# Gated mix of a recurrent memory attention and a 32-head attention: turns by transposing DMAs, zero products, paced weights, transfers issued by GpSimd

## The chip, the cores and the metric

One core of a Trainium2 chip. Its engines run their own instruction streams, in order, and meet at semaphores: TensorE (PE, with its weight loads PEld), VectorE (DVE), ScalarE (ACT), GpSimd (POOL) and SyncE (SP); transfers issued by SP, ACT or POOL run on the core's 16 DMA engines. The metric is the device time of one execution in microseconds, lower is better, as a median over runs.

## The reference

All inputs and the output are bfloat16.

```python
x = A_x                                            # [1, 2048, 576]
g = sigmoid((x * gate_w).sum(-1, keepdims=True))
return g * A(x) + (1 - g) * B(x)

def A(x):            # 64 segments of 32 rows, 32 heads of 128, memory of 8 rows
    mem = mem0
    for s in range(64):
        h = concat([mem, x[32*s : 32*s+32]])       # 40 rows x 576
        q, k, v = h @ Wq, h @ Wk, h @ Wv           # each 40 x (32 heads x 128)
        p = softmax(mask(q k^T / sqrt(128)))       # 40 x 40 for each head; memory rows see all
        o = (p v) @ Wo                             # 40 x 576
        mem = o[:8]                                # the next segment needs it
        out[s] = o[8:]

def B(x):            # 2048 rows, 32 heads of 18, no mask
    q, k, v = split(x @ wqkv)
    return softmax(q k^T / sqrt(18)) v @ wo
```

Both attentions work on `A_x`; `B_x` is not used. A is a recurrence: segment s+1 starts from eight rows that segment s ends with. B has no recurrence.

## The kernel before, in words

**Three stages.** (1) *Head*: x is loaded and turned, B's Q, K and V are projected (`project_qk` L528 on, `project_v`), evicted from PSUM and stored to DRAM in the layouts in which they are read back (`qtd`, `ktd`, `vgd`, `L561`, `L597`), while GpSimd loads A's weights wv, wq, wk (L478 and L481) in twelve chunks of 1 MB, each behind the one before the last. Then come the first 24 "last units" (`last_unit`, L803 and L807): the projections of the last 8 rows of 16 segments at once, which do not depend on the recurrence; their results are stored to `vld` and `qkd` (L841, L844). (2) *Segments*: the 64 steps of the recurrence, between whose instructions PE and ACT also do B's attention. (3) *Tail*: the last output products and stores.

**A segment.** The 8 memory rows and 24 of the x rows, 32 columns in all (`ht`), are multiplied with Wq, Wk, Wv in six units of 20 products (L1028; two halves of the heads for each), evicted to `tm` (L363). Q and K have to be turned, so that the head dimension lies on partitions: 16 PE transposes into a PSUM bank (L1087) and a DVE copy into `qk` (L1095). V goes to `v_sb` by eight small DMAs (L1067). GpSimd puts the 8 rows of the last units into `qk` (L997) and the next x rows into `ht` (L983 to L985). Then for each half: scores `psh` (L1108), exponent on ACT (L1118), mask, row sums `pss` (L1134), reciprocal, its broadcast `prb` (L1151), normalisation, `pso` (L1172), copies to `ot`, and 64 products with Wo into `acc` (L946). The memory rows of `acc` are cast (L1203, L1206), turned by three products `pw` (L1219 to L1221) and copied into the next `ht` (L1227).

**A visit** is one step of B's attention, 512 in all: scores `sb` of 128 keys and 512 queries of four heads (L708), their exponent `etb` on ACT (L717), and the product with V into `ob` (L726). Every 16 visits `ob` is normalised and stored. K, Q and V chunks are reloaded from DRAM through rings (`kch`, `qch`, `vch`, helper `by_head` L649).

**The order of the work** is set by a planner (`Plan`): every operation has an engine or two, a duration, dependences, a priority from the table `RANK`, and tokens for buffers; `run` simulates the engines and `choose` picks for each engine the ready operation of the best priority. The program is then written out in that order, so each engine's stream is fixed when it is built. `seg_gate` ties the visits to the segments: the first `RANK["ahead"]` visits may run before segment 0.

Of the kernel before, what the change touches and what calls it, by code (L numbers as in the profile page):

```python
# [17 lines left out]
    "switch": 0.289, "near": 0.006, "early": 0.149, "wait": 0.21, "Q0": 1.449, "K0": 1.44, "Q1": 1.668,  # L18
# [4 lines left out]
    "behind": 2, "tail": 0.042,  # L23
# [21 lines left out]
class Plan:  # L45
# [5 lines left out]
    SWITCH = 0.1  # L51

    def __init__(self):
        self.ops = []
        self.tokens = {}
        self.now = None
        self.lanes = [0.0] * self.LANES
        self.moved = 0.0

    def transfer(self, op):  # L60

        step = (op.end - op.start) / op.dmas
        for j in range(op.dmas):
            issued = op.start + (j + 1) * step
            self.moved = max(self.moved, issued + 0.9) + op.kb / op.dmas / 300.0
            self.lanes.append(max(self.moved + 1.0, self.lanes[-1]))
# [31 lines left out]
    def run(self):  # L98
# [12 lines left out]
        n = len(self.ops)  # L111
        best = {}
        dirty = set(free)
        while len(order) < n:
# [10 lines left out]
            est, op = best[pick]  # L125
            waiting_engs = op.engs
# [6 lines left out]
            if pick == "PE":  # L133
                if op.mode != mode:
                    dur += self.SWITCH
                mode = op.mode
            op.end = est + dur
            free[pick] = op.end
            if op.dmas:
# [20 lines left out]
    def choose(self, e, ops, now, mode):  # L160
        found = []
        for op in ops:
# [5 lines left out]
            if op.dmas:  # L168
# [47 lines left out]
def kernel(  # L216
# [37 lines left out]
    HD = H * Dh  # L254
    CT = 32
# [16 lines left out]

    const = ctx.enter_context(tc.tile_pool(name="const", bufs=1))
# [11 lines left out]
    nc.vector.memset(cap[:], 3.0e38)  # L285
    nc.vector.memset(bsel[:], 0.0)
# [24 lines left out]
    vgd = dpool.tile([GB, P, NKB * P], BF16, name="vgd")  # L311
    otd = dpool.tile([Dm, S], BF16, name="otd")
    vld = dpool.tile([n_seg * LO, HD], BF16, name="vld")
    qkd = dpool.tile([n_seg // SG, P, SG, 2, H * LO], BF16, name="qkd")
# [3 lines left out]
    def weights(name):  # L318
        return (
            aw1.tile([P, NF, HD], BF16, name=name + "_m"),  # L320
# [5 lines left out]
    def w_slice(w, c, f0, n):  # L326
        if c < NF:
            return w[0][:, c, f0:f0 + n], c
# [8 lines left out]
    wo7 = bint.tile([P, Dm], BF16, name="wo7")  # L337
# [50 lines left out]
    z_w7 = zero("zw7", wo7[:], 0.6, 4.0)  # L388
# [83 lines left out]
    weight_loads = {}  # L472
    chain = [wbl[-1], wbl[-1]]
    for w, src, name in ((wv, A_Wv, "wv"), (wq, A_Wq, "wq"), (wk, A_Wk, "wk")):
        w2 = src.rearrange("d h e -> d (h e)")
        for c in range(NF):
            def load_w(e, w=w, w2=w2, c=c):
                nc.gpsimd.dma_start(out=w[0][:, c, :], in_=rows(w2, c))  # L478
                for two in range(2):
                    o = TL * two + TR * c  # L480
                    nc.gpsimd.dma_start(  # L481
                        out=w[1][o:o + TR, :],
                        in_=w2[RW * c + P:RW * c + RW, two * (HD // 2):(two + 1) * (HD // 2)],
                    )

            chain.append(add(f"{name}{c}", "POOL", 2.1, load_w, [chain[-2]], prio=0.15, tail=8.5))
        weight_loads[name] = chain[-4:]
# [8 lines left out]
    gwl = add("gw", "POOL", 5.0, load_gw, [chain[5]], prio=0.9, tail=3.0)  # L496
# [35 lines left out]
    def project_qk(which, m, t, prio):  # L532
# [20 lines left out]

        def st(e):
# [15 lines left out]
    def project_v(hf, kb, prio):  # L570
# [24 lines left out]

        def st(e):
            dma(  # L597
                out=vgd[:, :, :].rearrange("g p (k f) -> k p g f", f=P)[kb][:, hf * GB // 2:(hf + 1) * GB // 2, :],
                in_=vt[:, :, :].rearrange("p (g j) e -> p g (j e)", j=4),
# [839 lines left out]
```

## Time and profile before

| | |
|---|---|
| time, median of 3 runs | 1567.85 us (1562.02 to 1577.5) |
| the profiled execution's own time | 1573.35 us |
| its span, first to last instruction | 1571.6 us |
| PE / ACT / DVE / POOL busy | 1425.7 / 1066.2 / 764.9 / 194.4 us |
| mean granted TensorE clock | 0.961 |
| first and last `pw` product (one for each of 63 segment ends) | 190.1 and 1514.0 us |

How to read it: a row of the page's part 5, or of the groups by line, is `line engine operation out<-in shapes xcount | busy, mean ns of one | idle time before, and what ended it`. A window row has for each engine its busy us and, in brackets, its instruction count, then the granted clock (1.00 is full speed), the DMA engines' busy share and GB/s. A timeline row is `start us, duration us, engine, line, operation, out<-in, forms, xcount, [idle before <-what ended it]`. "SPq" is SyncE's queue: it issues DMAs and is never counted as busy. Matmuls overlap their neighbours, so what one costs PE is best read from start to start.

### The profile page before, as it was taken

To read this page: it belongs to the slowest core of one execution; us is meant where nothing else is said; L and a number is where in the kernel's file an instruction comes from. 1 tells how busy PE (TensorE), PEld (TensorE's weight loads), DVE (VectorE), ACT (ScalarE), POOL (GpSimd) and SP (SyncE) were. 2 spreads that over 40 slices of the span, in tenths; PEclk is the share of its full clock that TensorE was granted. 3 is DMA by queue.
4 is the path that set the end of the run, shared out by engine and by line. 5 is a ranking of instruction groups with operands and counts; after the bars stand their busy time and mean duration, and the time that the engine had idled before them with its cause. 6 is when DMAs were issued, how large, how long until landed. Compare 5 with 4: busy or idle time off the path is not lost.

```text
span 1571.6 us, 68445 instructions
## 1 busy us (share of the span) xinstructions
PE 1425.7 (91%) x30582; PEld 813.4 (52%) x30582; DVE 764.9 (49%) x1604; ACT 1066.2 (68%) x809; POOL 194.4 (12%) x523
## 2 busy tenths in 40 slices
PE   5398999999999999999999999999999898988996
PEld 3154545555554545555555555555555454555555
DVE  5154555544545454545554544555444545443454
ACT  2121788877777777777777777777776767766771
POOL 7301000000000000010000000000110100000025
PEclk9599999999999999999999999999999999998998
DMA  9957411212222111222221112212131111111033
GB/s 319 287 152 206 68 44 51 56 33 45 42 49 49 32 44 53 56 43 46 39 50 44 42 43 52 57 39 41 38 76 37 34 34 40 33 32 31 26 106 97
DMA packets 246877, 104.83 MB, mean 67 GB/s; under 512 B 186487, under 2 KB 242039, under 8 KB 245047
## 3 DMA queue, kind: packets, MB, share of 16 engines
q1 hardware_dynamic: 241591, 80.40, 21.2%
q0 software_dynamic: 3840, 18.88, 3.5%
q8 instruction: 239, 3.92, 1.0%
q10 hardware_dynamic: 1152, 1.18, 0.3%
q14 instruction: 55, 0.45, 0.1%
HBM read 52.74 MB, written 30.86 MB: 53 GB/s over the span
## 4 chain that ended last, share of the span: by engine, by line
PE 72%; ACT 10%; DMA 7%; issue 4%; SPq 3%; DVE 3%; POOL 1%; ACTq 0%; DVEq 0%; POOLq 0%
PE pvv L1028 24%; PE acc L946 11%; PE sb L708 10%; ACT etb L717 9%; PE ob L726 8%; PE pt L1087 4%; PE pv L807 4%; DMA v_sb<-tm 3%; SPq L1067 2%; PE pq L539 2%; PE pso L1172 2%; PE pv L803 2%; PE psh L1108 1%; POOL wv_m L1349 1%; PE prb L1151 1%
## 5 line engine op out<-in xcount | busy, mean ns | idle before, releaser
L717 ACT ACTIVATE etb<-sb 128x2048 bf16<-128x2048 f32 x512 | 961.3, 1878 | 386.3 <-PE sb L708 328.2
L363 DVE CAST tm<-pvv 128x512 bf16<-128x512 f32 x352 | 242.6, 690 | 285.2 <-PE pvv L1028 270.9
L1028 PEld LDWEIGHTS <-ht 128*32 128x32 bf16 x7680 | 199.5, 96 | 186.9 <-DVE ht L1227 23.8
L708 PE MATMUL sb<-qch,kch 32*128 32x512 bf16 x2048 | 208.6, 391 | 28.9 <-ACT etb L717 18.0
L726 PE MATMUL ob<-etb,vch 128*32 128x512 bf16 x2048 | 207.4, 396 | 0.8 <-ACT etb L717 0.7
L946 PE MATMUL acc<-wo,ot 128*32 128x144 bf16 x8192 | 167.7, 245 | 10.9 <-issue 10.7
L946 PEld LDWEIGHTS <-ot 128*32 128x32 bf16 x8192 | 157.1, 107 | 22.2 <-issue 17.2
L1028 PE MATMUL pvv<-wk_m,ht 128*32 128x512 bf16 x2048 | 140.8, 380 | 18.3 <-DVE ht L1227 18.2
L1028 PE MATMUL pvv<-wq_m,ht 128*32 128x512 bf16 x2048 | 144.4, 380 | 0.0
L708 PEld LDWEIGHTS <-kch 32*128 32x128 bf16 x2048 | 65.1, 91 | 139.9 <-issue 109.3
L1028 PE MATMUL pvv<-wv_m,ht 128*32 128x512 bf16 x2048 | 133.9, 379 | 0.0
L983 POOL COPY ht<-xg 128x96 bf16<-128x96 bf16 x64 | 17.1, 267 | 859.7 <-PE pvv L1028 843.2
L363 DVE CAST ot<-pso 128x320 bf16<-128x320 f32 x197 | 90.0, 485 | 65.1 <-PE pso L1172 64.8
L1095 DVE COPY qk<-pt 128x1024 bf16<-128x1024 bf16 x128 | 87.8, 686 | 53.8 <-PE pt L1087 53.5
L726 PEld LDWEIGHTS <-vch 128*32 128x32 bf16 x2048 | 54.3, 93 | 112.6 <-issue 105.0
L1203 DVE CAST obf<-acc 128x144 bf16<-128x144 f32 x64 | 19.7, 307 | 169.4 <-PE acc L946 169.2
L1087 PEld LDWEIGHTS <-tm 128*128 128x128 bf16 x1024 | 57.5, 98 | 45.5 <-issue 27.1
L1087 PE MATMUL pt<-ident,tm 128*128 128x128 bf16 x1024 | 79.4, 220 | 0.0
L1172 PE MATMUL pso<-et,v_sb 64*128 64x40 bf16 x2048 | 54.7, 179 | 26.0 <-DVE ot L363 16.8
L1161 DVE TENSOR_TENSOR et<-et,prb 128x320 bf16<-128x320 bf16 x128 | 57.2, 483 | 23.8 <-PE prb L1151 22.1
L1172 PEld LDWEIGHTS <-v_sb 64*128 64x128 bf16 x2048 | 38.8, 94 | 56.3 <-DMA v_sb<-tm 29.0
L1247 POOL COPY otl<-ot 128x256 bf16<-128x256 bf16 x64 | 26.2, 409 | 328.2 <-DVE ot L363 187.8
(128 smaller groups left out, 1523.1 us busy)
## 6 DMA issues: line engine op xcount, KB each, us to landing
v_sb<-tm SPq DMA_DIRECT2D x512, 32.0 KB
qkd<-vl SPq DMA_DIRECT2D x64, 128.0 KB
xl<-qkd SPq DMA_DIRECT2D x64, 128.0 KB
wo<-in_A_Wo_dram POOLq DMA_DIRECT2D x4, 1152.0 KB, 11.3
wv_m<-in_A_Wv_dram POOLq DMA_DIRECT2D x4, 1024.0 KB, 10.6
vgd<-vt SPq DMA_DIRECT2D x32, 128.0 KB
wq_m<-in_A_Wq_dram POOLq DMA_DIRECT2D x4, 1024.0 KB, 10.1
wk_m<-in_A_Wk_dram POOLq DMA_DIRECT2D x4, 1024.0 KB, 12.3
```

The lines of the kernel that those rows point to most:

```text
L363: nc.vector.tensor_copy(out=out_of(), in_=in_of())
L539: nc.tensor.matmul(pq[:, :], lhsT=lw(c), rhs=xT[:, c, cs], start=(c == 0), stop=(c == NF))
L708: nc.tensor.matmul(sb[:, j, :], lhsT=kc[r, o:o + P], rhs=qt_[r, :], start=True, stop=True, tile_position=(32 * j, 0),)
L717: nc.scalar.activation(out=etb[:, :, :], in_=box["sb", gq, kb][:, :, :], func=ACT.Exp, scale=scale_b)
L726: nc.tensor.matmul(ob[32 * j:32 * j + 32, :], lhsT=vc[:, o + 32 * j:o + 32 * j + 32], rhs=etb[:, j, :], start=(kb == 0), stop=(kb == NKB - ...
L807: nc.tensor.matmul(pv[:, k * P:(k + 1) * P], lhsT=lw, rhs=xL[:, cc, cols], start=(c == 0), stop=(c == NF))
L946: nc.tensor.matmul(acc[32 * j:32 * j + 32, :], lhsT=o[:, slot, t0:t0 + CT], rhs=wo[:, h, RW * j:RW * j + RW], start=(first and s_ == 0), s ...
L1028: nc.tensor.matmul(pv[32 * j:32 * j + 32, :], lhsT=ht[:, cc, :], rhs=rw, start=(c == 0), stop=(c == NF), tile_position=(0, 32 * j), skip_g ...
L1087: nc.tensor.transpose(out=pt[:, a, :, i, :], in_=tm[:, i * Dh:(i + 1) * Dh], identity=ident[:, :])
L1095: nc.vector.tensor_copy(out=opened["qk"][:, hf, :, 0:16 * L].rearrange("p a (h t) -> p a h t", t=L)[:, :, :, 0:CT], in_=box["pt", s, hf][: ...
L1161: nc.vector.tensor_tensor(out=et[:, :], in0=et[:, :], in1=box["prb", s, hf][:, :], op=ALU.mult)
L1172: nc.tensor.matmul(ps[jj][:, r * L:(r + 1) * L], lhsT=v_sb[rr, hf * 1024 + r * Dh:hf * 1024 + (r + 1) * Dh], rhs=et[rr, r * L:(r + 1) * L] ...
```

## The change

1. **Turns.** The PE transposes of Q and K and the bank that they took are gone. Each of the four evicted `tm` tiles of a segment is turned by one transposing DMA on SP's queue from SBUF to SBUF (`tt`, three buffers), and a copy of half the former size (512 elements a row), on DVE or GpSimd, puts it into `qk`. In the built program 197 of these 256 copies stand on DVE and 59 on GpSimd.
2. **Zero products.** Where the planner sees PE idle for at least 0.216 us while an `ob` bank is open, it inserts products of a zero tile `nil` that add nothing to `ob`: 239 groups of four 32x512 (L767 in the new kernel) and 71 single 128x512 (L773).
3. **Weights** of A are loaded in the order and chunks of before, but each chunk waits (through a one-element DVE memset of its corner, `behind`) for an eviction of B's projections, and each row of 4096 is stored as four runs of 1024 elements (2 KB). Wo's four chunks wait for evictions of the last units in the same way.
4. **Issue.** K, Q and V reloads (all but the first ones), `otd`, `a_dram`, x rows and the later last units' stores are issued by GpSimd (`carrier`), in place of SP.
5. **DRAM layouts.** `vgd` is written in 1 KB rows in place of 256 B pieces; `qkd` is written in 1 KB rows in place of 64 B pieces and read back in 64 B pieces in place of 1 KB.
6. **One `otl` buffer** in place of two, `wo7` moved into the spare of wq and loaded near the end, and a new `RANK` table: among others projections go in the order Q0, K0, K1, Q1, V0, V1, and `psh` of the two halves stand apart.

```diff
-    "switch": 0.289, "near": 0.006, ... "Q0": 1.449, "K0": 1.44, "Q1": 1.668,
+    "switch": 0.563, "near": 0, ... "Q0": 0.487, "K0": 1.599, "Q1": 3.227,
...
+    def queue(e):
+        return nc.gpsimd.dma_start if e == "POOL" else nc.sync.dma_start
+    def carrier(n, far):
+        return ("POOL", 0.6 * n) if far else ("SP", 0.4 * n)
...
+            if pick == "PE" and open_ and self.warm is not None:
+                for m in ("col", "full"):
+                    if m not in (mode, op.mode):
+                        continue
+                    turn = 0.0 if mode == m else self.SWITCH
+                    done = sum(d for t, d in recent if t > free["PE"] - 2.5)
+                    if est - free["PE"] < self.WARM + turn + RANK["gap"] or done > RANK["cool"]:
+                        continue
+                    w = Op("warm", "PE", self.WARM, self.warm[m], [], 9.0, m, (), (), 0.0)
...
+    def behind(name, beat, corner, n, fn, deps, tail):
+        mark = add(f"mk{name}", "DVE", 0.07, lambda e: nc.vector.memset(corner(), 0.0), [beat, *deps], prio=0.05)
+        before = paced[-1:]
+        op = add(name, "POOL", 0.7 * n, fn, [mark, *deps, *before], prio=0.15, tail=5.5)
...
-                nc.gpsimd.dma_start(out=w[0][:, c, :], in_=rows(w2, c))
+                    nc.gpsimd.dma_start(
+                        out=w[0][:, :, c, :], in_=rows(w2, c).rearrange("p (b f) -> p b f", f=WB)
+                    )
...
+                    behind(f"{name}{c}", beats[2 + 4 * k], lambda w=w, c=c: w[0][0:1, 0, c, 0:1], 3, load_w, [], 5.5)
...
-        k_of[c] = add(f"lk{c}", "SP", 1.6, fn, [use, z_k[c % NKR], *stores_for(1, g, [kc])], prio=0.6, dmas=4, kb=90)
+        k_of[c] = add(f"lk{c}", *carrier(4, c >= 3), fn, [use, z_k[c % NKR], *stores_for(1, g, [kc])], prio=0.6, dmas=4, kb=90)
...
+    def warm_col(e):
+        for j in range(4):
+            nc.tensor.matmul(
+                box["ob"][32 * j:32 * j + 32, :], lhsT=nil[:, 0:32], rhs=unit[:, :].unsqueeze(1).to_broadcast([P, 4, P]), start=False, stop=False,
+                tile_position=(0, 32 * j), skip_group_check=True,
+            )
...
-            def turn(e, hf=hf, s=s):
-                box["pt", s, hf] = pt = bank([P, 2, 4, 4, CT], BF16, "pt")
-                for a in range(2):
-                    tm = box["tm", s, a, hf]
-                    for i in range(4):
-                        nc.tensor.transpose(
-                            out=pt[:, a, :, i, :], in_=tm[:, i * Dh:(i + 1) * Dh], identity=ident[:, :]
-                        )
+            for a, ev_a in ((0, eq), (1, ek)):
+                def turn(e, hf=hf, s=s, a=a):
+                    box["tt", s, a, hf] = tt = given(opened["fix"], "tt", [P, 4, P], BF16)
+                    nc.sync.dma_start_transpose(out=tt[:, :, :], in_=box["tm", s, a, hf][:, :])
...
+                def ct(e, hf=hf, s=s, a=a):
+                    eng = nc.vector if e == "DVE" else nc.gpsimd
+                    eng.tensor_copy(
+                        out=opened["qk"][:, hf, a, 0:16 * L].rearrange("p (j i t) -> p j i t", i=4, t=L)[:, :, :, 0:CT],
+                        in_=box["tt", s, a, hf][:, :, :].rearrange("p i (j t) -> p j i t", t=CT),
+                    )
```

Two places show what the planner made of it. On SP, late in the segments, one segment's rows before (`v_sb<-tm` are V's eight copies, `qch` a reload of Q, `xl` the last units' rows, `otd` and `a_dram` stores):

```order
L1067 DMA v_sb<-tm 32x512 x8
L649 DMA qch_125<-qtd 18x512 x4
L991 DMA xl<-qkd 128x512
L1006 DMA v_sb<-vld 8x2048 x2
L649 DMA otd<-stage 18x512 x4
L1236 DMA a_dram<-obf 24x4x144 x4
```

and SP's rows now, in the middle of the segments, from the place where B's output weights are loaded on:

```order
L1411 DMA xL<-in_B_wo_dram 128x4x576
L1412 DMA xL<-in_B_wo_dram 64x576
L1098 DMA v_sb<-vld 8x2048 x2
L1080 DMA xl<-qkd 128x16x32 x2
L1178 DMA_TRANSPOSE tt<-tm 128x4x128 x4
L1159 DMA v_sb<-tm 32x512 x8
```

The reloads and stores have left SP, and four transposing DMAs stand ahead of V's eight copies.

On DVE, one segment before from the copy into `ht` to the reciprocals (`et_1313` and `et_1315` are the exponents of half 0 and half 1):

```order
L1227 CAST ht_1304<-pw 128x6x8
L363 CAST tm<-pvv 128x512 x2
L1095 COPY qk<-pt 128x2x16x32
L363 CAST tm<-pvv 128x512 x2
L1095 COPY qk<-pt 128x2x16x32
L363 CAST tm<-pvv 128x512
L1124 TENSOR_TENSOR et_1315<-et_1315,cap 128x320
L1124 TENSOR_TENSOR et_1313<-et_1313,cap 128x320
L1143 RECIPROCAL rq<-pss 128x6 x2
```

and now (`et_1348` is half 0):

```order
L1322 CAST ht_1338<-pw 128x6x8
L412 CAST tm<-pvv 128x512 x4
L1187 COPY qk<-tt 128x16x32
L412 CAST tm<-pvv 128x512 x2
L1187 COPY qk<-tt 128x16x32
L1219 TENSOR_TENSOR et_1348<-et_1348,cap 128x320
L1238 RECIPROCAL rq<-pss 128x6
L1187 COPY qk<-tt 128x16x32
```

The first turned tile is now copied behind the fourth eviction, and the copy for half 1 stands behind half 0's mask and reciprocal: the two halves' softmax steps no longer follow each other in pairs.

More of the change, by code (lines that the diff above doesn't have):

```diff
@@ L51 @@
     SWITCH = 0.1
+    CROWDED = (28.0, 125.0)
+    WARM = 0.216
+    ARRAY = {"col": 1.0, "row": 1.0, "full": 0.9, "half": 0.3, "tall": 0.35}
     def __init__(self):
@@ L254 @@
     HD = H * Dh
+    WB = HD // NF
     CT = 32
```

231 lines of the change are left out of this document (146 added, 85 removed), and 8 rows, old and new, of the table RANK.

## The prediction

> **What bounds the kernel now.** I read the page first (shares, clock, chain), then cut the span into stages, then read the stages' waits and one segment's timeline. The page:
>
> ```profile
> span 1571.6 us, 68445 instructions
> PE 1425.7 (91%) x30582; PEld 813.4 (52%) x30582; DVE 764.9 (49%) x1604; ACT 1066.2 (68%) x809; POOL 194.4 (12%) x523
> PE 72%; ACT 10%; DMA 7%; issue 4%; SPq 3%; DVE 3%; POOL 1%; ACTq 0%; DVEq 0%; POOLq 0%
> ```
>
> PE is busy for 91% and is 72% of the chain that ended last. The average hides three stages, which the windows show (PE, PEld, DVE, ACT, POOL busy us; then clock, DMA share, GB/s), with the rows of the `pw` product that closes a segment, for the first 48 segments and the last 15:
>
> ```profile
> 20.00:80.00 60.00, 28.39 (x131) 14.52 (x131) 11.81 (x24) 4.52 (x4) 21.90 (x49) 0.72 0.96 313
> 80.00:127.00 47.00, 46.71 (x345) 24.08 (x343) 26.33 (x47) 10.46 (x8) 2.58 (x5) 1.00 0.52 147
> 127.00:169.00 42.00, 35.59 (x425) 24.55 (x422) 16.03 (x27) 13.06 (x7) 4.81 (x10) 0.92 0.81 192
> 190.00:1190.00 1000.00, 948.53 (x21829) 537.02 (x21826) 501.56 (x1053) 763.00 (x569) 87.10 (x283) 0.99 0.21 47
> 1190.00:1514.00 324.00, 293.40 (x6646) 165.47 (x6643) 154.15 (x326) 229.58 (x165) 27.42 (x87) 0.93 0.12 31
> 1514.00:1572.00 58.00, 43.64 (x725) 29.16 (x721) 27.97 (x57) 21.32 (x14) 29.56 (x21) 0.90 0.41 129
> L1221 PE MATMUL pw<-sel,bd x48: 166/166/168, 190.1 to 1188.5; 128*128 128x8 bf16 x48
> L1221 PE MATMUL pw<-sel,bd x15: 166/166/167, 1209.9 to 1514.0; 128*128 128x8 bf16 x15
> ```
>
> *Head*, to the first segment at 169: DMA-bound from 20 to 80 (share 0.96, PE 28 of 60 us at clock 0.72), PE-bound from 80 to 127 (46.7 of 47, DMA at 0.52), then the last units. *Segments with last units*: (1188.5 - 190.1) / 47 = 21.24 us each, PE idle (1000 - 948.5) / 47 = 1.1 us of it; PE's own work is the bound. *Segments without them*: (1514.0 - 1188.5) / 15 = 21.70 us each, longer though they have less to do; PE idles (324 - 293.4) / 15 = 2.0 us, and the clock of 0.93 takes 0.07 x 324 / 15 = 1.5 us more. There the chain through one segment and the clock bound it. *Tail*: 58 us.
>
> **The change, part by part.** *PE loses the turns.* Start to start, clock full, from two segments' PE:
>
> ```profile
> 810.34 1.03 PE L1028 MATMUL pvv<-wq_m,ht 128*32 128x512 bf16 x16
> 811.42 0.82 PE L1028 MATMUL pvv<-wq_m,ht 128*32 128x512 bf16 x12
> 816.63 0.62 PE L1087 MATMUL pt<-ident,tm 128*128 128x128 bf16 x8
> 817.18 0.40 PE L708 MATMUL sb<-qch,kch 32*128 32x512 bf16 x4
> 817.50 0.40 PE L726 MATMUL ob<-etb,vch 128*32 128x512 bf16 x4
> 817.73 1.04 PE L1028 MATMUL pvv<-wv_m,ht 128*32 128x512 bf16 x16
> 818.91 0.69 PE L1108 MATMUL psh<-qk 128*64 128x40 bf16 x32
> 819.62 0.40 PE L708 MATMUL sb<-qch,kch 32*128 32x512 bf16 x4
> ```
>
> One half's turns take 817.18 - 816.63 = 0.55 us, so 1.1 us a segment; a visit takes 817.73 - 817.18 = 0.55, a projection unit 811.42 - 810.34 = 1.08, `psh` of both halves 0.71. Where PE bounds, 1.1 us a segment is to be had. Against it I set 0.3 for what a new fixed order brings: the built order holds about 8.0 visits a segment there against 7.7 (0.2), and some waits grow. I take 0.8 x 47 = **38 us**.
>
> *The turn by DMA* has no row. What it must keep: in the new order Q1's unit is the last that is turned, and between it and half 1's `psh` stand V0, a visit, V1, half 0's `psh`, a visit, some last-unit pieces and row sums: 1.08 + 0.55 + 1.08 + 0.36 + 0.55 = 3.6 us, and about 1.2 more where last units fill in, 4.8. In that time must go the eviction, the turn T, the copy and the handing over:
>
> ```profile
> 1349.81 0.39 PE L1028 MATMUL pvv<-wv_t,ht 128*32 128x512 bf16 x4
> 1349.87 4.85 SPq L1067 DMA_DIRECT2D v_sb<-tm  x6
> 1350.28 0.69 DVE L363 CAST tm<-pvv 128x512 bf16<-128x512 f32 x1 [1.04 <-PE pvv L1028]
> 1356.04 0.31 PE L1172 MATMUL pso<-et,v_sb 64*128 64x40 bf16 x7 [0.30 <-DMA v_sb<-tm]
> L1067 SPq DMA_DIRECT2D v_sb<-tm x512: 507/588/1834, 177.9 to 1530.3; - x171
> 163.52 0.69 DVE L363 CAST vl<-pv 128x512 bf16<-128x512 f32 x1 [1.59 <-PE pv L807]
> 167.89 0.69 DVE L363 CAST vl<-pv 128x512 bf16<-128x512 f32 x1 [0.81 <-DMA qkd<-vl]
> L1095 DVE COPY qk<-pt 128x1024 bf16<-128x1024 bf16 x128 | 87.8, 686 | 53.8 <-PE pt L1087 53.5
> L997 POOL COPY qk<-xl 128x256 bf16<-128x256 bf16 x128 | 52.9, 440 | 69.0 <-DMA xl<-qkd 30.1 <-PE psh L1108 19.5 <-POOL ht L985 12.1
> ```
>
> The eviction is done 1350.97 - 1349.81 = 1.16 us after its last product starts, 0.95 after the unit's slot; the half-size copy is half of 686, 0.35 (on GpSimd twice 440, 0.9, for 59 of 256); 0.1 to PE. So T may be about 3.4 us with last units and 2.2 without. Its bounds: the 32 KB copy issued last of six (at 1349.87 + 4.85 - 0.59 = 1354.13) was in use at 1356.04, so 1.9 us from below; a store of the same 128 KB in its smallest pieces freed its buffer (one of three, used in turn) 167.89 - 164.21 = 3.7 us after the eviction, so 3.7 from above. A turn moves 2-byte elements between partitions, which is nearer to the small pieces: I take 3.0. That costs nothing in segments with last units and 0.8 us in the others. At 1.9 those are free; at 3.7 the cost is 0.3 and 1.5 us.
>
> The Trainium skill prices it otherwise: "VectorE: DVE Perf Modes", section "The three transpose paths", has 1309 ns for a 128x128 turn through the DMA crossbar and advises TensorE where PSUM will do. This turn is four such blocks, so an estimate from that page is 5.2 us; no run here shows it, and by it `psh` would wait 1.8 and 3.0 us, and the sum would be 1.8 x 47 + 3.0 x 15 - 12 = 118 higher.
>
> *Zero products*: 239 groups of 0.216 us (1.08 / 5) and 71 of as much are 67 us of PE time if none lay in idle time. They stand where PE waits for DVE, such as between `acc` and `pw`, and the two stages idle 51 + 31 us; I price them at nothing, with 20 us as the bound for those that miss. What they can bring is the clock:
>
> ```profile
> PE sb L708 <- issue: 1.4, 1, 1.4
> ```
>
> This is the longest wait of PE among the last segments, 1.4 us, and still the clock there is 0.93. "TensorE: Matmul & The Clock Gate", in the Trainium skill, asks in "Why this matters for your kernels" only that no idle gap exceed about 3 us; by that rule there would be nothing to repair and the sum would lack the next 15 us. The row speaks for many short gaps, so I count two thirds of 1.5 us a segment.
>
> *Segments without last units* then gain 1.1 (turns) + 1.0 (clock) + 0.3 (about 7.1 visits in place of 7.6, at 0.55) - 0.8 (T) = 1.6 us, x 15 = **24 us**; between 0.9 and 2.4 by T's ends.
>
> *Head.* Weights and stores no longer compete in one burst:
>
> ```profile
> ACT stg L361 <- DMA qtd<-stg: 25.9, 1, 25.9
> DVE vt L363 <- DMA vgd<-vt: 21.3, 1, 21.3
> 137.98 1.87 PE L803 MATMUL pv<-wv_m,xL 128*128 128x512 bf16 x4 [4.71 <-DVE vl L363]
> ```
>
> Evictions stood 26 and 21 us behind their stores while weights filled the DMA engines, and the last units 4.7 us behind theirs. The bytes stay, so B's projections cannot end before the DMA time that they need: 0.96 x 60 + 0.52 x 47 = 82 us after 20, at 102 in place of 127, and not later than now. I take half, 12 us, and 10 of the 42 us of the last-unit stage, whose 64 B stores become 1 KB rows: **22 us**; the bounds are 50, and 5 lost if a paced weight comes late. Reading `qkd` back in 64 B pieces is prefetched a segment ahead on engines at share 0.21: nothing.
>
> *Issue by GpSimd*:
>
> ```profile
> L481 POOL DMA_DIRECT2D wv_t<-in_A_Wv_dram x8: 484/492/522, 17.4 to 29.4; - x8
> SPq L649 <- PE sb L708: 71.9, 24, 7.1
> SPq L649 <- DVE stage L764: 50.1, 17, 5.5
> ```
>
> About ten issues a segment at 0.49 us join 87.1 / 47 = 1.9 us of copies on an engine with 20 us: no bound. But SP's waits for a visit or for `stage` (up to 7.1 us) now stand on GpSimd, and behind them its copies into `qk` and `ht`; SP in turn is free for turns. I take nothing, and price a miss below. *Tail*: less than 2 us, from a visit or two less; `wo7`'s load is small and early enough.
>
> **Sum**: 1573.35 - 38 - 24 - 22 - 2 = 1487 for the profiled execution; the median lies 5.5 below it, so **1481 us**.
>
> **Rivals.** (a) *The turns come late* (slower). Add to the 3.7 us of the small pieces the longest stall that SP's issue of `v_sb` shows, 1834 - 588 ns, or 1.25: with T = 5.0, half 1's `psh` waits 1.6 us in the 47 segments and 2.8 in the 15, 117 us against my 12 for T, so 1481 + 105 = 1586. Each 0.1 us more of T adds 62 x 0.1 = 6, so it gives up all the gains at T = 4.7 and is slower by 1% from 5.0. It decides sooner if turns pass one after another, for then half 1's two wait for half 0's. For it: no row shows a turn. Against: SP's 32 KB copies follow each other every 0.6 us. (b) *The chain, not PE, bounds everywhere*, and PE's freed 1.1 us becomes waiting: only clock and half of the head stay, 1568 - 15 - 11 = 1542. For it: segments with less work are the longer ones. Against: 948 of 1000 busy. (c) *GpSimd falls behind its order*: half of its 41 inherited waits, 3 us each, land on a segment's path: +60, 1541. (d) *More is gained*: half of PE's 1.1 us of waits goes too (26 us), the head gives 50: 1481 - 26 - 28 = 1427. (e) That it does not do what it says: the built order holds 256 turns, so only the zero products can miss, +20, 1501, inside my own range.
>
> **Chances.** A measurement here tells about 1%, 16 us, from no change. My case with (e), 1450 to 1525: 0.50; (d) 0.12; (b) and (c) 0.18, of which 0.13 are still faster by 1% and 0.05 are no change; a weak (a) that ends within 1%: 0.03; (a) as slower: 0.17. So faster 0.75, same 0.08, slower 0.17. The range is 1420 to 1590: it takes in (b), (c), (d) and T's ends, and leaves out what of (a) lies above it, about 0.12, and 0.05 below.
>
> **What would show it.** Right: no PE `pt`, `pw` rows about 20.4 us apart to the 48th and 20.1 after, the clock above 0.97 from 1190 on, first segment near 147, and PE's idle before `psh` small. T too high: PE or DVE idle at `qk` or `psh` for the DMA `tt<-tm`. (c): GpSimd's `qk` copies late and `psh` waiting for them. The prediction is wrong if turns queue on SP, or if the head stays at 169 because the bytes bound it.

## The result and the profile after

The changed kernel takes 1519.0 us (median of 4 runs, 1516.6 to 1521.9) beside 1572.7 us for the kernel before on the same chip: a ratio of 0.967, with a 95% interval of 0.960 to 0.973. The forecast was 1481 us with a range of 1420 to 1590: faster, as forecast, by 54 us in place of 87. The profiled execution took 1516.6 us. Of the kernels below, one execution, the profiled one of `nozero` (1554.1 us), was in a slower state of the chip and is left out of its median.

The page of the new kernel, its totals and its chain of waits:

```profile
span 1514.9 us, 69086 instructions
PE 1404.0 (93%) x30585; PEld 767.0 (51%) x30585; DVE 753.8 (50%) x1735; ACT 1051.5 (69%) x765; POOL 574.6 (38%) x1207
PE 63%; DMA 13%; ACT 12%; SPq 4%; issue 3%; DVE 3%; POOL 2%; ACTq 0%; DVEq 0%; POOLq 0%
```

PE is as busy as before and yet on less of the chain: 63% in place of 72%, with DMA up from 7 to 13%. The windows of the new kernel by its stages (PE, PEld, DVE, ACT, POOL busy, clock, DMA share, GB/s), and the rows of the `pw` product that closes a segment, once before and once from the 48th segment end on:

```profile
20.00:80.00 60.00, 47.92 (x314) 24.41 (x314) 23.98 (x54) 6.42 (x7) 23.58 (x49) 0.83 0.79 255
80.00:127.00 47.00, 41.69 (x277) 20.68 (x276) 21.28 (x41) 12.86 (x9) 7.75 (x18) 0.93 0.65 223
127.00:179.00 52.00, 47.38 (x812) 29.67 (x808) 21.85 (x47) 33.19 (x21) 12.54 (x25) 0.93 0.71 189
190.00:1159.00 969.00, 919.31 (x21485) 504.10 (x21488) 498.04 (x1144) 745.58 (x521) 379.98 (x814) 1.00 0.36 73
1159.00:1458.00 299.00, 282.55 (x6721) 147.83 (x6712) 141.17 (x331) 220.42 (x163) 99.33 (x216) 0.98 0.31 61
L1316 PE MATMUL pw<-sel,bd x47: 166/166/167, 178.7 to 1140.3; 128*128 128x8 bf16 x47
L1316 PE MATMUL pw<-sel,bd x16: 166/166/167, 1159.8 to 1458.5; 128*128 128x8 bf16 x16
```

Set against the rows of before (190.1, 1188.5, 1514.0, span 1571.6), the 56.7 us come from four places:

| stage | before | after | gained | forecast |
|---|---|---|---|---|
| to the first `pw` | 190.1 | 178.7 | 11.4 | 22 |
| 47 segments with last units | 998.4 (21.24 each) | 981.1 (20.87) | 17.3 | 38 |
| the last 15 segments | 325.5 (21.70) | 298.7 (19.91) | 26.8 | 24 |
| tail | 57.6 | 56.4 | 1.2 | 2 |

Two terms fell short, those of the 47 segments and of the head. In the 47 segments PE is busy for 919.3 / 969 = 0.949 of the time, the same share as before (948.5 / 1000). But the zero products are a part of it. Their two lines alone, in the same two stretches (PE busy, PEld busy, clock, DMA share, GB/s; the first two rows are L767, the second two L773):

```profile
190.00:1159.00 969.00, 41.88 (x524) 13.46 (x528) 1.00 0.36 73
1159.00:1458.00 299.00, 24.91 (x328) 8.50 (x330) 0.98 0.31 61
190.00:1159.00 969.00, 10.23 (x37) 2.69 (x37) 1.00 0.36 73
1159.00:1458.00 299.00, 8.87 (x27) 1.86 (x27) 0.98 0.31 61
```

In the first stretch that is 52.1 us, 1.1 us for each of its 46.4 segments: as much as the turns took of PE before. (They overlap their neighbours; the time in which only they keep PE busy is about 0.7 us a segment.) So the larger part of the time that the turns gave back is there, filled with products that compute nothing. Why it could not be used is the question of the first experiments.

The head shows the other shortfall. The first segment's projections start at 134 us, 34 us earlier than before and 13 earlier than forecast, but this segment takes 44 us. The chain of waits of the new kernel between 130 and 180 us (start, us, what), and the timeline row with which the segment starts:

```profile
134.43 1.04 PE L1120 MATMUL pvv<-wq_m,ht 128*32 128x512 bf16 x16
...
153.98 0.70 DVE vl L412
...
154.70 8.41 DMA qkd<-vl
...
163.18 2.73 DMA xl<-qkd
...
166.03 0.41 POOL qk L1089
...
166.48 0.62 PE psh L1203 x8
```

The first `psh` waits for the last of the first 24 last units (`vl` at 153.98), for its store (8.4 us to land), the reading back (2.7 us) and GpSimd's copy. The segment started early and then waited for rows that were not ready.

### The profile page after: what moved, and what is told of

Same layout as the page of the kernel before. It is cut to its first block, busy times and chain, and to the rows that moved or that the text cites. A ratio compares the mean times of both kernels' runs of the same rounds, so it can differ in the third digit from the quotient of the medians.

```text
span 1514.9 us, 69086 instructions
## 1 busy us (share of the span) xinstructions
PE 1404.0 (93%) x30585; PEld 767.0 (51%) x30585; DVE 753.8 (50%) x1735; ACT 1051.5 (69%) x765; POOL 574.6 (38%) x1207
## 4 chain that ended last, share of the span: by engine, by line
PE 63%; DMA 13%; ACT 12%; SPq 4%; issue 3%; DVE 3%; POOL 2%; ACTq 0%; DVEq 0%; POOLq 0%
PE pvv L1120 25%; ACT etb L804 11%; PE sb L795 10%; PE acc L1034 8%; PE ob L813 7%; DMA v_sb<-tm 5%; SPq L1159 3%; PE pv L894 3%; DMA tt<-tm 2%; PE pq L602 2%; PE ob L767 2%; PE pv L890 2%; DMA vgd<-vt 2%; PE psh L1203 1%; PE pso L1267 1%
## 5 line engine op out<-in xcount | busy, mean ns | idle before, releaser
L412 DVE CAST tm<-pvv 128x512 bf16<-128x512 f32 x382 | 263.7, 691 | 297.9 <-PE pvv L1120 297.1
L1120 PEld LDWEIGHTS <-ht 128*32 128x32 bf16 x7680 | 204.7, 97 | 187.3 <-DVE ht L1322 11.5
L1034 PE MATMUL acc<-wo,ot 128*32 128x144 bf16 x8192 | 161.6, 228 | 10.0 <-issue 9.3
L1034 PEld LDWEIGHTS <-ot 128*32 128x32 bf16 x8192 | 137.2, 98 | 29.9 <-issue 16.7
L1187 POOL COPY qk<-tt 128x512 bf16<-128x512 bf16 x59 | 36.8, 625 | 279.2 <-DMA tt<-tm 279.1
L412 DVE CAST ot<-pso 128x320 bf16<-128x320 f32 x179 | 83.4, 484 | 87.2 <-PE pso L1267 86.9
L1187 DVE COPY qk<-tt 128x512 bf16<-128x512 bf16 x197 | 63.6, 323 | 36.3 <-DMA tt<-tm 35.6
L1089 POOL COPY qk<-xl 128x256 bf16<-128x256 bf16 x128 | 50.4, 403 | 81.2 <-PE psh L1203 70.4
L716 POOL DMA_DIRECT2D qch<-qtd x120 | 61.0, 515 | 42.6 <-PE sb L795 39.0
L716 POOL DMA_DIRECT2D kch<-ktd x116 | 58.9, 514 | 45.1 <-PE sb L795 22.2
L716 POOL DMA_DIRECT2D otd<-stage x124 | 62.3, 509 | 36.0 <-DVE stage L856 34.9
```

Of the source, the lines that this page charges most:

```text
L412: nc.vector.tensor_copy(out=out_of(), in_=in_of())
L716: dma(out=rows_, in_=pads) if out else dma(out=pads, in_=rows_)
L1034: nc.tensor.matmul(acc[32 * j:32 * j + 32, :], lhsT=o[:, slot, t0:t0 + CT], rhs=wo[:, h, RW * j:RW * j + RW], start=(first and s_ == 0), s ...
L1089: nc.gpsimd.tensor_copy(out=opened["qk"][:, f, :, 0:16 * L].rearrange("p a (h t) -> p a h t", t=L)[:, :, :, CT:L], in_=box["xlt", s][:, :, ...
L1120: nc.tensor.matmul(pv[32 * j:32 * j + 32, :], lhsT=ht[:, cc, :], rhs=rw, start=(c == 0), stop=(c == NF), tile_position=(0, 32 * j), skip_g ...
L1187: eng.tensor_copy(out=opened["qk"][:, hf, a, 0:16 * L].rearrange("p (j i t) -> p j i t", i=4, t=L)[:, :, :, 0:CT], in_=box["tt", s, a, hf] ...
```

## The experiments

Each kernel is the changed one, or the one before, with the edit shown. Times are medians of 4 runs or more beside runs of the kernel before on the same chip (`nozero` of 3, `light` is one run). First `pw`, the mean distance of `pw` rows over the 47 segments and over the last 15, and the clock granted from 190 to 1150 and from 1150 to 1450 us are from each one's trace, a single execution; for `nozero` that is its longest, 1554.1 us.

| kernel | median us | ratio to before | first `pw` | 47 segments | last 15 | clock |
|---|---|---|---|---|---|---|
| before | | 1 | 190.1 | 21.24 | 21.70 | 0.99, 0.93 |
| changed | 1519.0 | 0.967 (0.960 to 0.973) | 178.7 | 20.87 | 19.91 | 1.00, 0.98 |
| nozero | 1535.8 | 0.976 (0.969 to 0.983) | 183.1 | 21.29 | 20.74 | 0.97, 0.90 |
| halfexp | 1514.3 | 0.960 (0.956 to 0.965) | 182.2 | 20.82 | 19.72 | 0.99, 0.99 |
| lalite | 1527.1 | 0.970 (0.965 to 0.974) | 181.9 | 21.02 | 19.89 | 0.99, 0.99 |
| light | 1519.3 | | 185.4 | 20.77 | 19.93 | 0.88, 0.93 |
| peturn | 1599.5 | 1.015 (1.011 to 1.019) | 176.5 | 21.95 | 21.37 | 1.00, 0.99 |
| tfree | 1517.5 | 0.965 (0.960 to 0.970) | 180.3 | 20.88 | 19.90 | 1.00, 0.99 |
| b_turn | 1649.1 | 1.049 (1.042 to 1.056) | 200.9 | 22.39 | 22.07 | 0.95, 0.92 |
| sp_issue | 1595.0 | 1.015 (1.009 to 1.022) | 180.2 | 22.29 | 20.59 | 0.99, 0.99 |
| b_turn_pool | 1610.0 | 1.021 (1.018 to 1.023) | 197.5 | 21.94 | 21.65 | 0.96, 0.90 |
| b_zero | 1576.6 | 1.001 (0.998 to 1.004) | 192.0 | 21.63 | 20.84 | 0.99, 0.99 |
| unpaced | 1530.5 | 0.975 (0.969 to 0.981) | 186.5 | 20.88 | 19.94 | 1.00, 0.98 |
| qkd_old | 1533.2 | 0.975 (0.970 to 0.980) | 193.3 | 21.00 | 19.96 | 1.00, 0.98 |

### What bounds a segment

The theories were P, PE's own work (the prediction's), and V, a bound that the prediction had not seen: a visit's scores, exponent and next scores follow each other through one buffer, 2.43 us at the least, and about 7.9 visits a segment make 19.2 of 20.87 us.

**halfexp** shortens that cycle:

```diff
-nc.scalar.activation(out=etb[:, :, :], in_=box["sb", gq, kb][:, :, :], func=ACT.Exp, scale=scale_b)
+nc.scalar.activation(out=etb[:, 0:2, :], in_=box["sb", gq, kb][:, 0:2, :], func=ACT.Exp, scale=scale_b)
...
-rhs=etb[:, j, :],
+rhs=etb[:, j % 2, :],
```

> The changed kernel, but each exponent of a visit covers 1024 of the 2048 columns, and both halves of the value product read these; the output is not the reference's. PE's work and every order stay. The exponent falls from 1.88 to about 1.0 us. Theory V (the visits' cycle bounds): the least cycle falls from 2.43 to about 1.6 us, PE's own 18.8 us of work without zero products and its waits for the recurrence bound next, so the 47 segments fall from 20.87 to about 19.8 and the whole by 50 us or more, below 1470. Rival P (PE's work bounds, zero products included): 47 segments stay within 0.2 us of 20.87, the whole within 10 us of 1519.

**lalite** takes PE work away:

```diff
+                    if q > 0 and 0 < k < NF:
+                        return
...
-                for c in range(NF + 1):
+                for c in (range(NF + 1) if q == 0 else (0, NF)):
```

> The changed kernel, but the last units inside the segments do only the first and the last of their five partial products; the output is not the reference's. That takes about 3/5 of 1.97 us, 1.1 us, of PE from each of the 47 segments, nothing else moves. Rival P (PE's work bounds): 47 x 1.1 = 52 us less, 1467. Theory V (the visits' cycle bounds): at most 10 us less. The last 15 segments stay in both.

The windows of halfexp (first two rows) and of lalite, 190 to 1150 and 1150 to 1450 us:

```profile
190.00:1150.00 960.00, 911.60 (x21288) 494.08 (x21296) 494.11 (x1142) 438.01 (x517) 380.90 (x815) 0.99 0.37 73
1150.00:1450.00 300.00, 281.24 (x6736) 144.35 (x6729) 141.91 (x333) 132.52 (x163) 100.26 (x218) 0.99 0.33 61
```

```profile
190.00:1150.00 960.00, 871.13 (x20460) 469.39 (x20468) 491.96 (x1132) 733.92 (x512) 379.45 (x811) 0.99 0.38 72
```

ACT's busy share went from 745.6 / 969 = 0.77 to 0.46 and the segments by 0.05 us; V fell. PE's went from 0.949 to 871.1 / 960 = 0.907, which is 0.9 us a segment, and the mean segment did not get shorter (20.87 to 21.02; the median one went from 20.68 to 20.40, with more long ones beside it). The 52 us that P had for it did not come; P fell too. With every engine's order kept, neither of the two busiest engines sets the pace alone. That left theory C: the chain of steps through one segment, which less work elsewhere does not shorten. **light** makes nearly all work between these steps small at once (its last units are those of lalite):

```diff
-sb[:, j, :], lhsT=kc[r, o:o + P], rhs=qt_[r, :], start=True, stop=True,
+sb[:, j, 0:P], lhsT=kc[r, o:o + P], rhs=qt_[r, 0:P], start=True, stop=True,
...
-nc.scalar.activation(out=etb[:, :, :], in_=box["sb", gq, kb][:, :, :], ...)
+nc.scalar.activation(out=etb[:, :, 0:P], in_=box["sb", gq, kb][:, :, 0:P], ...)
...
-ob[32 * j:32 * j + 32, :], lhsT=..., rhs=etb[:, j, :],
+ob[32 * j:32 * j + 32, :] if kb == 0 else ob[32 * j:32 * j + 32, 0:P], lhsT=...,
+rhs=etb[:, j, 0:P].unsqueeze(1).to_broadcast([P, 4, P]) if kb == 0 else etb[:, j, 0:P],
```

> The changed kernel with the work between a segment's steps made small and every order kept: a visit's scores, exponent and value product cover 128 of 512 queries (the first of sixteen apart), the last units in the segments do two of five partial products; the output is not the reference's. PE loses about 7.9 x 0.35 + 1.1 = 3.9 us a segment, ACT 7.9 x 1.4 = 11. Theory C (the recurrence's own chain is nearly as long as the segment): the 47 segments stay at 19.5 us or more. Theory F (the chain is short, and the work put between its steps in PE's order is what makes the segment long): 17 us or less, with PE's waits not above 2 us a segment.

The window of light, and the chain of waits by line from 190 to 1150 us, for the kernel before, the changed one and light (the view cuts each row off at its end; `pt` are the turns on PE, `etb`, `sb` and `ob` the visits):

```profile
190.00:1150.00 960.00, 853.93 (x20655) 502.61 (x20663) 492.82 (x1141) 279.46 (x516) 380.21 (x812) 0.88 0.39 73
by line: PE pvv L1028 28.2%; PE acc L946 12.3%; PE sb L708 12.2%; PE ob L726 9.8%; ACT etb L717 8.7%; PE pt L1087 5.1%; PE pv L807 4.6%; issue 3.4%; DMA v_sb<-tm 2.9%; PE pv L803 2.3%; PE pso L1172 2.2%; PE psh L1108 1.8%; SPq L1067 1.6%; P
by line: PE pvv L1120 28.5%; ACT etb L804 11.8%; PE sb L795 11.1%; PE acc L1034 9.0%; PE ob L813 8.3%; DMA v_sb<-tm 5.6%; SPq L1159 3.8%; issue 3.6%; DMA tt<-tm 2.9%; PE pv L894 2.6%; PE ob L767 2.0%; PE pv L890 1.9%; PE pso L1267 1.4%; PE 
by line: PE pvv L1123 22.8%; PE acc L1037 16.5%; DMA tt<-tm 11.5%; DMA v_sb<-tm 8.8%; SPq L1162 5.4%; issue 4.1%; PE ob L813 4.0%; PE sb L795 3.8%; DVE tm L412 3.5%; PE pso L1270 3.0%; PE ob L767 3.0%; PE prb L1249 1.9%; DVE qk L1190 1.0%; 
```

The segments stay at 20.77 us, the whole at 1519.3, as C had it. The visits' rows fall from 31% of the chain to 8% (`etb` no longer shows in the row), and the links of the segment's own steps, the turns (2.9 to 11.5%), V's copies and `acc`, take their place: several chains of nearly equal length lie side by side. The granted clock fell to 0.88 in it, which stretches the PE links of the chain; if all of PE's busy time were stretched, that is 0.12 x 853.9 / 46.2 segments = 2.2 us, so at full clock the chain would still be 18.6 us or more. F's 17 us is out. How much of 20.87 the chain alone makes, between 18.6 and 20.8, this one run can't tell.

### The turns

**peturn** puts the turns back on PE in the changed kernel:

```diff
-nc.sync.dma_start_transpose(out=tt[:, :, :], in_=box["tm", s, a, hf][:, :])
+for i in range(4):
+    nc.tensor.transpose(out=pt[:, a, :, i, :], in_=tm[:, i * Dh:(i + 1) * Dh], identity=ident[:, :])
```

> The changed kernel with the turns back on PE (16 transposes, one PSUM bank, the DVE copy of 1024 elements as before), planned with the changed kernel's table; all other parts stay. Rival P: 62 segments get 1.1 us longer, 68 us, about 1587. Theory V: PE's 1.1 us takes the place of zero products in the 47 segments, which gain or lose less than 0.3 us each; only the last 15, where the chain through a segment counts, may change, by -0.7 to +1.1 us each: 1495 to 1550. If the turns by DMA come late at some place, this is faster than 1519.

It is 80 us slower than the changed kernel, and slower than the kernel before. The 47 segments are 1.08 us longer, the last 15 by 1.46: what P had priced, for another reason. The turn stands on PE between the projections and `psh`, so its 1.1 us are a link of the chain: in the kernel before it is 5.1% of the chain (the row above), 1.1 us a segment. (51 + 22 us of the 80 are in the segments; its tail is 10 us longer, for a reason that is open.) The table was made for turns by DMA, so this is not the price of PE turns in an order of their own.

**tfree** asks whether the turn by DMA is itself a link:

```diff
-in_=box["tt", s, a, hf][:, :, :].rearrange("p i (j t) -> p j i t", t=CT),
+in_=opened["wo"][:, 0, 0:4 * P].rearrange("p (i j t) -> p j i t", i=4, t=CT),
```

> The changed kernel, but the copies into qk read a constant tile in place of the turned tile, so no copy waits for a turn or for the evictions of Q and K; the transposing DMAs are still issued and their result is unused, the output is not the reference's, the order of every engine stays. Theory C (the chain through one segment bounds, with several links of nearly equal length): the turns' 2.9% of the chain between 190 and 1150 us go, but the next link is close behind, 5 to 25 us less than 1519. Theory T (the turns come late, and that is where the forecast gain went): 47 x 0.4 us or more, 20 to 50 us less, and the 47 segments at or below 20.45 us. If the turns are hidden: within 5 us of 1519.

Nothing changes: 20.88 and 19.90 us. The turn is hidden. What it takes, from the changed kernel's timeline and the group of all 256:

```profile
808.12 0.69 DVE L412 CAST tm<-pvv 128x512 bf16<-128x512 f32 x1 [1.54 <-PE pvv L1120]
808.84 5.74 SPq L1178 DMA_TRANSPOSE tt<-tm  x4
809.86 0.69 DVE L412 CAST tm<-pvv 128x512 bf16<-128x512 f32 x1 [1.05 <-PE pvv L1120]
812.33 0.29 DVE L1187 COPY qk<-tt 128x512 bf16<-128x512 bf16 x1 [0.70 <-DMA tt<-tm]
813.06 0.61 POOL L1187 COPY qk<-tt 128x512 bf16<-128x512 bf16 x1 [8.51 <-DMA tt<-tm]
L1178 SPq DMA_TRANSPOSE tt<-tm x256: 1188/1214/2600, 136.5 to 1467.4; - x128
```

From the first eviction's end (808.81) to the copy that waits for its turn are 3.5 us, from the second's (810.55) 2.5 us. Over the whole trace a turn's semaphore events come 2.4 us after its issue in the median (of the 222 turns whose events can be told apart; 2.3 at the least, mostly below 4.6). Each turn holds SP for 1.2 us, twice a plain copy's 0.59.

### Who issues

**b_turn** is the kernel before with the DMA turns alone:

```diff
+nc.sync.dma_start_transpose(out=tt[:, :, :], in_=box["tm", s, a, hf][:, :])
...
-opened["otl", i] = fix.tile([P, H, 4 * LO], BF16, name=f"otl{i}")
+opened["otl"] = fix.tile([P, H, 4 * LO], BF16, name="otl")
```

> The kernel before with the turns by transposing DMAs alone (and the one otl buffer and the moved wo7, without which the three turn buffers find no room), planned with the old table. The prediction's price: 0.8 x 47 us for PE's freed time and 1.1 - 0.8 us x 15 in the last segments, 43 us less than before, a ratio of 0.973. Theory C (the chain bounds, and the old order has psh right behind the turn): the turn of 3.5 us with its handing over takes the place of 0.55 us of transposes and 0.69 us of copy, so most of the 1.1 us is waited away: ratio 0.985 to 1.03.

Far worse than either theory: 4.9% slower than before. Its SP queue in one segment that takes 32 us, and the two `psh` of that segment (timeline rows):

```profile
650.02 2.50 SPq L1080 DMA_TRANSPOSE tt<-tm  x2
652.62 0.54 SPq L676 DMA_DIRECT2D vch<-vgd  x1
653.21 5.01 SPq L1061 DMA_DIRECT2D v_sb<-tm  x8
658.32 0.53 SPq L969 DMA_DIRECT2D xg<-xtd  x1
658.90 0.51 SPq L970 DMA_DIRECT2D xg<-xtd  x1
659.45 0.60 SPq L971 DMA_DIRECT2D xg<-xtd  x1
660.15 1.82 SPq L648 DMA_DIRECT2D kch<-ktd  x4
662.07 1.23 SPq L1080 DMA_TRANSPOSE tt<-tm  x1
```

```profile
654.48 0.43 PE L1105 MATMUL psh<-qk 128*64 128x40 bf16 x16
...
665.15 0.62 PE L1105 MATMUL psh<-qk 128*64 128x40 bf16 x16
```

The fourth turn is issued 9.5 us after the third's end, behind eight copies of V, the x rows and a K reload, and half 1's `psh` follows 10.7 us after half 0's. A fourth turn that comes more than 3 us behind the third stands in 3 of the 47 segments, which take 30.1 us in the mean, the others 21.9; these three are some 25 of the 75 us. **sp_issue** does the reverse, the changed kernel with its far transfers back on SP:

```diff
-return ("POOL", 0.6 * n) if far else ("SP", 0.4 * n)
+return ("SP", 0.4 * n)
```

> The changed kernel with all the transfers that it gave to GpSimd issued by SP again, planned with the same table. SP then issues 10 more of 0.4 to 0.6 us in a segment beside 4 turns of 1.2 us and 8 copies of V of 0.59, some 17 of 20.9 us, and its waits for a visit or for a stage stand ahead of turns. Theory C: turns and V's copies come later, 0.3 us a segment or more, 20 to 60 us more than 1519. The prediction's view (the issuing engine costs nothing): within 10 us of 1519.

76 us slower than the changed kernel, 67 of them in the 47 segments, by the same picture: the window of a long segment has the fourth turn behind a store of `otd`, V's copies and the x rows. The fourth turn is late in this way in 7 of the 47 segments (28.9 us in the mean, the others 21.1), which makes 54 of the 67 us; in the changed kernel and in b_turn_pool it is late in none. (The order of every engine was planned anew here, with 1814 single zero products in place of 1027, so not all of the 76 us need be the queue's.)

```profile
452.61 3.83 SPq L1178 DMA_TRANSPOSE tt<-tm  x3
456.54 1.52 SPq L716 DMA_DIRECT2D otd<-stage  x4
458.16 5.28 SPq L1159 DMA_DIRECT2D v_sb<-tm  x8
...
465.37 1.24 SPq L1178 DMA_TRANSPOSE tt<-tm  x1
469.58 0.43 PE L1203 MATMUL psh<-qk 128*64 128x40 bf16 x16 [2.01 <-DVE qk L1187]
```

**b_turn_pool** gives the kernel before both, the turns and the issue by GpSimd (the edit is b_turn's and the change's `carrier`).

> The kernel before with the turns by transposing DMAs (as in the run on the turns alone) and with the far transfers issued by GpSimd, old table, no zero products, weights and layouts as before. Theory S (the turns are slow only where other transfers stand ahead of them on SP): the ratio falls from 1.049 to 1.00 or less. Theory O (the old order, with psh right behind the turn and two halves side by side, is what makes them late, whoever issues): it stays above 1.03.

The ratio falls from 1.049 to 1.021, about half-way: giving the far transfers to GpSimd is worth some 40 us here, and what remains is neither S's 1.00 nor O's 1.03. What remains may be the old order or the clock, which is 0.96 and 0.90 here; these were not told apart.

### The zero products

**nozero** leaves them out of the changed kernel and keeps every order:

```diff
-            op.fn(op.eng)
+            if op.name != "warm":
+                op.fn(op.eng)
```

> The changed kernel with its 310 zero products left out and every other instruction in the same order. In the new profile they take 0.98 us of PE in each of the 47 segments with last units and 2.0 us in each of the last 15. Theory V (the visits' own cycle bounds: scores, exponent of 1.88 us, next scores, at least 2.43 us for each of about 7.9 visits a segment): the freed time becomes waiting, the 47 segments stay at 20.9 us each and the whole within 1% of 1519. Rival P (PE's own work bounds, and the zero products are a part of it): 47 x 0.98 + 15 x 2.0 = 76 us less, 1443. Rival K (they hold the clock): the granted clock from 1160 on falls from 0.98 to about 0.93 and the last 15 segments take 1.5 us more each, 22 us in all, 1541.

17 us slower (1530.3, 1535.8 and 1548.9 against 1519.0), near K's 22. Its windows are from the profiled execution, the longest (1554.1 us); two rows from one of its segments and its longest wait of PE among the segments stand below them:

```profile
190.00:1150.00 960.00, 880.46 (x20276) 490.37 (x20293) 485.36 (x1117) 724.50 (x503) 375.22 (x798) 0.97 0.35 71
1150.00:1450.00 300.00, 270.31 (x6211) 148.95 (x6204) 136.67 (x323) 215.46 (x160) 99.62 (x218) 0.90 0.34 63
1229.40:1236.30 6.90, 6.09 (x121) 2.96 (x113) 3.63 (x10) 5.87 (x5) 3.00 (x9) 1.00 0.33 78
1236.40:1243.20 6.80, 6.42 (x141) 4.22 (x141) 3.96 (x9) 5.19 (x5) 2.98 (x7) 0.50 0.38 67
PE sb L796 <- ACT etb L805: 30.3, 72, 2.0
```

Without them the clock is 0.97 and 0.90 in this execution. The mean over the whole execution was 0.948 to 0.958 in the three others, against 0.980 to 0.985 in the four of the changed kernel, so the drop is in all of them. It comes in steps: between the first and the last `pw` of this trace the clock is at half speed in 27 stretches of 3.4 or 6.8 us, 130 us together, in the changed kernel in 4, 17 us together. The stretch of the last window row began after 12 us in which PE had no wait above 0.3 us. So on balance the products that fill the waits bring 17 us here by holding the clock. K had the place wrong: in this trace more is lost in the 47 segments (0.42 us each, 20 us) than in the last 15 (0.83 us each, 12 us).

**b_zero** inserts them into the kernel before by the same rule (the lines of `Plan.run` that the change shows, `nil`, `unit`, and the two functions).

> The kernel before with the zero products alone, placed by the same rule in its own order, with its own table. If they hold the clock whatever the order: the granted clock rises from 0.96 to 0.98 or more, the last 15 segments lose 1 us each and the others 0.2 us: about 25 us less, a ratio of 0.984. If they miss the gaps, their PE time lies on the path: ratio 1.00 to 1.03.

The clock rises from 0.93 to 0.99 in the late stretch and the last 15 segments fall by 0.86 us each, but the 47 others grow by 0.39: 13 us against 18, no gain. (The distances are from its profiled execution, which is 6 us above the median.) That fits products that lie on the path in the old order, where PE had turns to do; which of them do was not shown.

### The head

**unpaced** loads the weights in the old chain, and **qkd_old** restores the layout of the last units:

```diff
-weight_loads[name].append(behind(f"{name}{c}", beats[2 + 4 * k], lambda ..., 3, load_w, [], 5.5))
+chain.append(add(f"{name}{c}", "POOL", 2.1, load_w, [chain[-2]], prio=0.15, tail=8.5))
+weight_loads[name].append(chain[-1])
```

> The changed kernel with A's weights loaded in one chain, each chunk behind the one before the last, as before, in runs of 2 KB; Wo's chunks behind the last of them. If the pacing brought the head's 11.5 us: the first pw at about 190 in place of 178.6, the whole 8 to 20 us more than 1519, and evictions of B waiting 20 us and more for their stores. If the layouts and the order brought it: within 5 us of 178.6 and of 1519.

```diff
-queue(e)(out=qkd[q][kind * 8 + hf * 4 + j], in_=vl[:, :])
+queue(e)(out=qkd[q][:, :, kind, o:o + 4 * LO], in_=vl[:, :].rearrange("p (s f) -> p s f", s=SG))
```

> The changed kernel with qkd in its old layout: stored in 64-byte pieces, read back in rows of 1 KB. The chain from 130 to 180 us of the new profile lies for 15 us on the stores of qkd and for 3 us on the reload in 64-byte pieces. If the 1 KB rows are what made the head shorter: the first pw 5 us later or more. If they hold nothing: the first pw within 3 us of 178.6, and the segments within 0.1 us of 20.87 and 19.9.

The first `pw` moves to 186.5 and 193.3 us, the whole by 11 and 14 us, and the segments hardly move. Kernels whose edit leaves the head's weights and layouts alone have their first `pw` between 176.5 and 185.4, so the layout's 14.6 us stand clear of that spread, and the pacing's 7.8 do not. The whole is clearly longer for both (1525.4 to 1537.0 and 1528.9 to 1535.2 us, against 1516.6 to 1521.9). So the old layout alone takes back the 11.4 us that the head gained; how much of it is the pacing's is not settled.

## Why the prediction was right or wrong

**The 47 segments: the step that failed.** "PE's own work is the bound" and "Where PE bounds, 1.1 us a segment is to be had" gave 38 us; 17.3 came. The step read a PE that is 95% busy as the bound. halfexp and lalite show that it is not in the changed kernel: taking away 0.9 us of PE, or 0.9 us from each exponent, leaves the mean segment at 20.8 to 21.0, and light, which takes away both and more, at 20.77. PE was full because an order had been built that puts other work into the waits of the recurrence, and the chain through a segment is nearly as long as that full PE (between 18.6 and 20.8 us by light). For the kernel before no run shows this; it is inferred from the changed one. Rival (b), "the chain, not PE, bounds everywhere", described this stage, but it drew the wrong consequence, that the freed 1.1 us brings nothing: the turns were themselves a link of the chain (5.1% of it before; peturn, 1.08 us a segment). Against the gain stands what the rest of the change and its order cost: peturn's 21.95 is 0.71 us above the kernel before, where the prediction had set 0.3 us "for what a new fixed order brings", and 1.08 - 0.71 = 0.37 us is what was measured. How the 0.71 divides is open: peturn's order was planned with a table made for turns by DMA, and the zero products, which cost 0.39 us a segment in the old order (b_zero), may be a part of it.

**The last 15 segments** came out right in size, 26.8 for 24, and in part by luck. The turn was charged 0.8 us a segment there (12 us) and cost nothing (tfree). Against peturn the turns gave 1.46 in place of 1.1. The clock rose as assumed, from 0.93 to 0.98; leaving the zero products out makes these segments 0.83 us longer in nozero's longest execution, for the 1.0 that was set. These sizes add up to more than the 1.79 us a segment that came, so something else took some of it back; what, is open.

**The turn's duration** was taken as 3.0 us between bounds of 1.9 and 3.7. It is 2.4 in the median, 3.5 and 2.5 in the rows shown, so inside the bounds and a little shorter than assumed. Rival (a) had the wrong condition: not a long T made turns late in the runs in which they were late, but a queue, as b_turn and sp_issue show; "the prediction is wrong if turns queue on SP" had named it. "VectorE: DVE Perf Modes" in the Trainium skill, section "The three transpose paths", has 1309 ns for one 128x128 block; this case's 128x512 was in use after 2.5 and 3.5 us, not after four times that.

**The issue by GpSimd** was the largest term that the prediction priced at nothing: taken back alone, it is 76 us with the order that this brings. "SP in turn is free for turns. I take nothing" named the reason and gave it no number. A part of the price was within reach: SP's own rows had eight copies of 0.59 us and some ten far issues a segment, and four turns had to pass between the eviction and `psh`. Rival (c), GpSimd behind its order, did not occur: in the changed kernel's trace the weight loads of `psh` wait for GpSimd's copies of turned tiles 15 times, 7.0 us in all, where (c) had 60.

**Zero products**: their PE time was priced at nothing, with 20 us for those that miss, and the clock that they hold at 15 us; on balance they are worth 17 us, clock and PE time together. The prediction decided by its row, where the longest wait of PE was 1.4 us and the clock still 0.93. nozero agrees, with no wait above 2.0 us in the segments and a clock of 0.90. The Trainium skill's "TensorE: Matmul & The Clock Gate" asks in "Why this matters for your kernels" for no idle gap above about 3 us; by these rows that is no safe limit here. The same page of the Trainium skill tells in Part 1, "A second HAM failure mode", of frequent small idles between groups of products that make the clock swing; nozero's 27 stretches at half clock agree with it.

**The head**: 11.4 for 22. The projections ended earlier than assumed (the first segment began at 134, not 147), but "the last-unit stage, whose 64 B stores become 1 KB rows" was still the last thing that the first segment waits for. The step took the start of the first segment for the time at which it can go through.

**The sum** had the right sign, and the time lies in its range. Of its four terms two held in size (last segments, in part by luck, and tail), and two were twice too large: the 47 segments, for the bound that was misread, and the head. That the change is faster at all rests on a term priced at nothing, the issue by GpSimd: without it the kernel is slower than before (sp_issue, a ratio of 1.015).

## What to carry to other kernels

An engine that is 95% busy under an order built to fill every wait is no proof that its work is the bound: ask what a segment would take if that work were gone, and price an edit by the links it takes out of the chain, not by the busy time it frees. Parts that work through one queue have to be priced together: with the far transfers on another engine the turns by DMA were worth 80 us against PE turns planned with the same table, and put alone into the old kernel they cost 75 us (1649.1 against 1574.2). Time that can't be used may still be filled with products that compute nothing, where the granted clock falls with the waits.

## What was not expected of the hardware

- The granted clock fell to 0.90 in a stretch in which PE was busy 270 of 300 us and never waited for more than 2.0 us (nozero's longest execution), in steps to half speed of 3.4 or 6.8 us; with products of a zero tile in the waits it was 0.98. Taking the turns off PE without them also lowered it (b_turn, 0.95 from 190 to 1150 us, for 0.99 before).
- A transposing DMA of 128x512 elements keeps the issuing queue for 1.2 us, and the next one can follow right behind: four in 5.7 us, the first of them in use 3.5 us after its issue, the second 2.5 us.
- With `qkd` written in 64-byte pieces and read in 1 KB rows, the first segment ended 15 us later than with 1 KB rows written and 64-byte pieces read (193.3 against 178.7 us; other kernels lie between 176.5 and 185.4). The reading in 64-byte pieces took 2.7 us on the chain of the first segment; the later segments were not shorter without it (21.00 and 19.96 us).
